# A new order for the opening of an attention-and-feed-forward kernel: five blank matmuls of full width and the six small ones taken out, copies shared anew between ScalarE and VectorE, keys of pair 2 turned before those of pair 1, and the first load of w_in held on other rows

## The chip, the cores and the metric

The kernel runs on one core of one Trainium2 chip. The metric is the device time of one execution in microseconds (us); a kernel's time is the median of several executions.

## The reference

The inputs q, k and v have 4 batches, 8 heads, 768 positions and 64 channels. Each query sees the keys nearer than 16 positions, and beside them one summary key and value for each of the 24 blocks of 32 positions. The result of attention, 3072 tokens by 512, goes through two matrix products with a swish between them.

```python
k_sum = k.reshape(B, H, nb, 32, D).max(axis=3)
v_sum = v.reshape(B, H, nb, 32, D).mean(axis=3)
scores_l = where(|i - j| < 16, scale * q @ k.T, -1e9)
scores_s = scale * q @ k_sum.T + log(32)
a = softmax(concat([scores_l, scores_s], -1))
x = (a @ concat([v, v_sum], 2)) -> (B * S, H * D)       # 3072 x 512
h = x @ w_in                                            # 512 x 2048
out = (h / (1 + exp(-beta * h))) @ w_out                # 2048 x 512
```

## The kernel before

**Units.** The eight heads are four pairs g = 0..3; the two heads of a pair lie on the two halves of the 128 partitions. Keys and queries are needed with the channel on the partitions, so they are turned. The tiles kT (keys), qn (queries), km (summary keys), e (exponentials) and xT (the result, turned) are in bf16. The 64-position tile m of the queries meets 96 keys around it and the 24 summary keys, on 120 of 128 partitions, so one exponential (L437) covers both parts of the softmax. The values are in two layouts: ve begins each tile of 128 rows 16 positions earlier than the tile, and vo holds the same rows shifted by 64. A product of e with ve or vo, one column of which is ones, gives the values and the sum by which they are divided (normalization, L527 and L528). After that x is turned (L535), multiplied with w_in (tile w_in_sb, result h in h_sb after the swish on ScalarE), and h with w_out.

**Stages.** Four batches follow one another. Attention of batch b + 1 is spread between the matmuls of batch b. Only the attention of batch 0 has nothing to hide behind. It is the *head* of the kernel, some 30 us, and does the first 384 positions (u = 0) of all four pairs and the scores of the other half (u = 1); the values of that other half come later, between the matmuls (`av0`).

**The order in the head** is written out by hand in the list HEAD: each entry is one step, and a step's instructions go to the end of their engine's queue in the order of the list. Each engine works through its own queue and waits for what an instruction needs. The steps:

- `blank n w`: n matmuls of zeros, w columns wide, into bank one[1] (L727). They compute nothing.
- `kt g x`, `qt g x`: 16 small transposes of the keys or queries of pair g into bank x (L374). `kc g e`, `qc g e`: the copy of the turned rows into kT or qn; the engine e is 'a' ScalarE (L358), 'd' VectorE (L361) or 'p' GpSimd (L364).
- `km g`: the maximum over each block of 32 keys, on VectorE (L351).
- `vc g e`: the cast of the loaded rows of v (tile vst) to bf16 in ve (L446). `vu g e`, `vl g e`: small copies from ve into vo, of 64 and of 32 rows.
- `sm g x`: seven matmuls for the summary values. `mc g e`: their copy into vm_one.
- `sc g u x`: the scores (L405 the summary keys, L407, L412 the tiles of 64, L416). `ex g u`: the exponential.
- `av g x`: the values of u = 0 (L509 with vm_one, L515 with ve and vo). `no g`: normalization. `xt g x`, `xc g e`: turning x and its copy into xT.
- `wi i`: the load of the i-th quarter of w_in, 512 columns, on GpSimd's DMA queue (L321). `begin`: the first matmuls with w_in (L568). `silu`: the load of ScalarE's table for the swish (L730).

**Loads in the head.** The rows of k and q are loaded on GpSimd's DMA queue, which turns them to bf16 on the way (krow, qrow): the heads of pair 0, of pair 1, and of pairs 2 and 3 together. Those of v go on SyncE's queue. `behind(a, b)` makes the load a wait until the load b has landed: v of pair 1 stands behind the third load of k, and the first quarter of w_in behind v of pair 1 (`vl[1]`).

**The order after the head.** The matmuls of the feed-forward part are a list of steps, `main`; everything beside it is put in by the table AT. Its numbers are positions in `main`: 6.199 means after step 6 of that list, in the order of the fractions. `av0` holds the values of batch 0's other half (pairs 0 and 1, then 2, then 3), `hs0` and `hs1` to `hs3` the sums of parts of h (tile s_sb, L635) that the second product needs (it is done by seven products in place of eight, so sums of h and w_out are formed on VectorE), `mk` the masking of the exponentials, `sc` the scores, `av` the values, `exp` and `silu` the table loads.

## Time and profile before

| what | value |
|---|---|
| time, median of 3 runs | 218.96 us (218.94, 218.96, 219.5) |
| the profiled execution, its own time | 219.06 us |
| its span, first to last instruction | 217.4 us |
| granted TensorE clock, mean | 1.0 |
| TensorE matmul (PE) busy | 205.4 us, 94% |
| TensorE weight load (PEld) busy | 141.9 us, 65% |
| VectorE (DVE) busy | 140.7 us, 65% |
| ScalarE (ACT) busy | 119.4 us, 55% |
| GpSimd (POOL) busy | 61.1 us, 28% |
| chain that ended last, by engine | PE 52%, DVE 21%, DMA 7%, SyncE's queue 6%, ACT 5%, issue 4%, POOL 3% |

Times in the rows of the trace are microseconds from the start of the span. A row of a timeline has the start, the busy time of the row, the engine, the source line, the operation, the tile written and the tile read with their shapes, and the number of instructions that the row holds. In square brackets stands the idle time of the engine ahead of the row and what ended it. In the chain of waits each row is one step of the work that ended last, followed back from the end. The blank matmuls count as busy time of TensorE, so the 94% says nothing on useful work in the head.

### The profile page before, as it was taken

The page shows a single profiled execution, that of the slowest core. Times are in us where ns is not written, and L with a number is a line of the kernel's source. Part 1 is how long each engine was busy: PE and PEld are TensorE (multiplying, and loading weights), DVE is VectorE, ACT ScalarE, POOL GpSimd, SP SyncE. Part 2 cuts the span into 40 slices and gives each one's busy share as a digit, 9 for nine tenths or more (in the row PEclk, how much of TensorE's full clock was granted, in tenths as well). Part 3 has the DMA queues.
Part 4 walks back from the last instruction along what each step waited for, and adds up shares of the span by engine and source line. Part 5 has one row for each costly group of instructions (what it writes and reads, how often), then busy time and mean ns, then how long its engine had stood idle before and what let it go on. Part 6 is the DMA issues. An engine that isn't in the chain of part 4 may idle for free.

```text
span 217.4 us, 5803 instructions
## 1 busy us (share of the span) xinstructions
PE 205.4 (94%) x2407; PEld 141.9 (65%) x2407; DVE 140.7 (65%) x323; ACT 119.4 (55%) x183; POOL 61.1 (28%) x93
## 2 busy tenths in 40 slices
PE   7978989899998899999999899999999999999993
PEld 2457756566544477556788785566878865568882
DVE  4286753599956995277899950599979713363222
ACT  2235777558669511676876143967981409663210
POOL 7617393001260004535240116163510110000111
PEclk9999999999999999999999999999999999999999
DMA  6999979999837999999959979999950740000242
GB/s 123 189 232 158 207 102 181 203 207 216 152 103 190 234 167 186 250 214 181 197 106 281 187 187 259 222 205 206 146 152 18 159 132 0 0 0 3 97 96 100
DMA packets 78394, 33.93 MB, mean 156 GB/s; under 512 B 60688, under 2 KB 75424, under 8 KB 78368
## 3 DMA queue, kind: packets, MB, share of 16 engines
q1 hardware_dynamic: 61968, 23.92, 52.2%
q0 software_dynamic: 7424, 7.34, 21.2%
q10 hardware_dynamic: 8976, 2.30, 7.0%
q8 instruction: 19, 0.31, 0.6%
q14 instruction: 7, 0.06, 0.1%
HBM read 27.37 MB, written 6.29 MB: 155 GB/s over the span
## 4 chain that ended last, share of the span: by engine, by line
PE 52%; DVE 21%; DMA 7%; SPq 6%; ACT 5%; issue 4%; POOL 3%; DVEq 0%; POOLq 0%
PE big L590 18%; PE one L654 9%; PE acc L654 7%; DMA kT<-kn 5%; PE big L568 4%; PE one L727 4%; DVE e L441 4%; DVE kw L361 2%; ACT e L437 2%; SPq L562 2%; DVE w_out_sb L327 2%; DVE qn L361 2%; DMA kst<-in_k_dram 2%; PE one L605 2%; DVE xn L528 2%
## 5 line engine op out<-in xcount | busy, mean ns | idle before, releaser
L590 PE MATMUL big<-xT,w_in_sb 128*128 128x384 bf16 x360 | 60.5, 326 | 0.0
L590 PEld LDWEIGHTS <-w_in_sb 128*128 128x128 bf16 x384 | 37.5, 98 | 25.1 <-issue 0.7
L601 ACT ACTIVATE h_sb<-big,beta_sb 128x768 bf16<-128x768 f32 x45 | 39.6, 904 | 25.9 <-PE big L590 25.8
L654 PEld LDWEIGHTS <-h_sb 128*128 128x128 bf16 x320 | 30.8, 98 | 4.5
L635 POOL TENSOR_TENSOR o_sb<-p,u 128x256 f32<-128x256 f32 x10 | 7.3, 727 | 90.0 <-DVE u L635 75.1
L437 ACT ACTIVATE e<-big,bias 128x768 bf16<-128x768 f32 x32 | 27.4, 900 | 6.6 <-PE big L416 4.5
L654 PE MATMUL one<-w_out_sb,h_sb 128*128 128x256 bf16 x240 | 30.2, 273 | 0.1
L654 PEld LDWEIGHTS <-s_sb 128*128 128x128 bf16 x240 | 23.1, 98 | 2.9
L635 DVE TENSOR_TENSOR s_sb<-h_sb 128x768 bf16<-128x768 bf16 (+2 forms) x16 | 8.5, 529 | 21.8 <-ACT h_sb L601 21.7
L635 DVE TENSOR_TENSOR u<-one,p 128x256 f32<-128x256 f32 x20 | 8.4, 420 | 14.9 <-PE one L654 14.7
L446 POOL CAST ve<-vst 128x832 bf16<-128x832 f32 (+1 forms) x15 | 13.3, 900 | 15.3 <-DMA vst<-in_v_dram 12.8
L358 ACT COPY o_sb<-one 128x256 f32<-128x256 f32 (+1 forms) x14 | 6.1, 434 | 19.1 <-PE one L654 10.1
L441 DVE TENSOR_TENSOR e<-e,mask 128x768 bf16<-128x768 bf16 x24 | 13.4, 586 | 3.5 <-ACT e L437 3.2
L605 PE MATMUL one<-w_out_sb,h_sb 128*128 128x512 bf16 x64 | 15.2, 381 | 0.0
L355 POOL COPY kw<-km 128x288 bf16<-128x288 bf16 x12 | 7.6, 636 | 20.5 <-DVE km L347 14.3
L351 DVE TENSOR_REDUCE km<-kT 128x24 bf16<-128x768 bf16 x12 | 11.3, 943 | 2.7 <-ACT kT L358 2.7
L528 DVE TENSOR_TENSOR xn<-big,r 128x768 bf16<-128x768 f32 (+1 forms) x14 | 12.6, 900 | 0.5
L568 PE MATMUL big<-xT,w_in_sb 128*128 128x384 bf16 x64 | 11.6, 327 | 0.8 <-ACT xT L358 0.8
L727 PE MATMUL one<-blank 128*128 128x512 bf16 (+1 forms) x32 | 10.0, 457 | 1.3 <-DVE blank L230 1.3
L558 POOL CAST qn<-qst 128x768 bf16<-128x768 f32 x8 | 7.5, 944 | 12.9 <-DMA qst<-in_q_dram 6.8
L654 PE MATMUL acc<-t_sb,h_sb 128*128 128x256 bf16 x80 | 10.9, 273 | 0.0
L820 ACT ACTIVATE h_sb<-big,beta_sb 128x384 bf16<-128x384 f32 x16 | 8.3, 578 | 4.4 <-PE big L568 4.4
(149 smaller groups left out, 316.2 us busy)
## 6 DMA issues: line engine op xcount, KB each, us to landing
out_dram<-o_sb SPq DMA_DIRECT2D x19, 256.0 KB, 2.7
vst<-in_v_dram SPq DMA_DIRECT2D x13, 336.0 KB, 4.8
kst<-in_k_dram SPq DMA_DIRECT2D x8, 384.0 KB, 5.3
qst<-in_q_dram SPq DMA_DIRECT2D x8, 384.0 KB, 4.9
w_in_sb<-in_moe_w_in_dram POOLq DMA_DIRECT2D x4, 512.0 KB, 8.2
w_out_sb<-in_moe_w_out_dram POOLq DMA_DIRECT2D x4, 512.0 KB, 12.7
vo<-ve SPq DMA_DIRECT2D x12, 107.2 KB, 2.3
vst<-in_v_dram SPq DMA_DIRECT2D x3, 416.0 KB, 7.3
```

What stands on the lines that cost most here:

```text
L351: nc.vector.tensor_reduce(out=km[g][:, NK:NK + nb], in_=kT[g][:, W:W + S].rearrange("p (n f) -> p n f", f=block), op=ALU.max, axis=AX.X)
L437: nc.scalar.activation(out=e[:], in_=s[:, :, 0:HS], func=ACTF.Exp, bias=bias[:, 0:1], scale=scale)
L441: nc.vector.tensor_mul(out=e.rearrange("p h (m q) -> p h m q", q=QT), in0=e.rearrange("p h (m q) -> p h m q", q=QT), in1=(mask2 if b > 1 e ...
L446: eng.tensor_copy(out=ve[:, g, lo:hi, 0:D], in_=vst[g][:, lo:hi])
L528: nc.vector.tensor_mul(out=x[:, 3 * us[0]:3 * us[0] + 3 * n].rearrange("p (k j) h d -> p k (j h) d", k=n), in0=tv[:, :, :, 0:D], in1=r[:, ...
L568: nc.tensor.matmul(t[:, 0:HS], w_in_sb[:, ki, i * P:(i + 1) * P], xT[:, ki, 0:HS], start=(ki == 0), stop=(ki == k1 - 1))
L590: nc.tensor.matmul(o, w_in_sb[:, ki, i * P:(i + 1) * P], x, start=(ki == 0), stop=(ki == k1 - 1))
L601: nc.scalar.activation(out=o, in_=t, func=ACTF.Silu, scale=beta_sb[:, i:i + 1])
L605: nc.tensor.matmul(t[:, 0:hi - lo], h_sb[:, n, ms * P:(ms + 1) * P], w_out_sb[:, n, lo:hi], start=(n == 0), stop=(n == k2 - 1))
L635: eng.tensor_tensor(out=o, in0=a, in1=b, op=op)
L654: nc.tensor.matmul(SLOTS[n], a[:, j, t * P:(t + 1) * P], b[:, j], start=(j == 0 and n not in (2, 3, 7)), stop=(j == J2 - 1), skip_group_ch ...
L727: nc.tensor.matmul(t, blank[:, 0:P], blank[:, 0:t.shape[-1]], start=True, stop=True)
```

## The change

The list HEAD is written anew, some fifty numbers of AT change, and the loads of the head get a table of their order (FIRST) and of what each held load stands behind (HOLD). The computation and the sizes of all instructions that remain are the same, but for one cast of v (pair 3): its first part, 7 of 13 columns, moves from VectorE to GpSimd.

```diff
 AT = {
...
-    'av0': [1.99, 3.682, 6.199],
+    'av0': [1.99, 3.661, 4.754],
...
-    'hs0': [34.279, 36.98, 42.604, 40.178],
+    'hs0': [36.284, 36.98, 42.604, 40.783],
...
 HEAD = [
-    ('blank', 9, 512), ('beta',), ('blank', 5, 512), ('kt', 0, 0), ('kc', 0, 'a'), ('km', 0), ('blank', 6, 512),
-    ('kt', 1, 1), ('kc', 1, 'a'), ('blank', 6, 512), ('kt', 2, 6), ('blank', 2, 256), ('kc', 2, 'd'), ('kt', 3, 6),
-    ('vc', 0, 'p'), ('vu', 0, 'd'), ('qt', 0, 2), ('kc', 3, 'a'), ('sm', 0, 7), ('mc', 0, 'a'), ('vl', 0, 'p'),
-    ('km', 1), ('qc', 0, 'd'), ('vc', 1, 'p'), ('qt', 1, 5), ('km', 2), ('blank', 2, 256), ('sc', 0, 0, 0),
-    ('vu', 1, 'p'), ('wi', 0), ('ex', 0, 0), ('qc', 1, 'd'), ('sc', 1, 0, 1), ('blank', 2, 256), ('qt', 2, 5),
-    ('qt', 3, 0), ('ex', 1, 0), ('qc', 2, 'd'), ('av', 0, 2), ('qc', 3, 'a'), ('km', 3), ('no', 0), ('sc', 2, 0, 2),
-    ('sc', 0, 1, 0), ('ex', 0, 1), ('sm', 1, 6), ('mc', 1, 'a'), ('vl', 1, 'd'), ('xt', 0, 7), ('vc', 2, 'd'),
-    ('ex', 2, 0), ('av', 1, 6), ('no', 1), ('xc', 0, 'd'), ('sc', 3, 0, 2), ('sm', 2, 6), ('wi', 1),
-    ('vc', 3, 'p', 7, 13), ('vl', 2, 'a'), ('ex', 3, 0), ('mc', 2, 'd'), ('sc', 1, 1, 0), ('vc', 3, 'd', 0, 7),
-    ('vu', 2, 'a'), ('ex', 1, 1), ('wi', 2), ('xt', 1, 4), ('xc', 1, 'd'), ('av', 2, 7), ('sc', 2, 1, 2), ('wi', 3),
-    ('ex', 2, 1), ('no', 2), ('sm', 3, 2), ('mc', 3, 'a'), ('sc', 3, 1, 0), ('ex', 3, 1), ('vu', 3, 'd'),
-    ('vl', 3, 'p'), ('xt', 2, 5), ('xc', 2, 'a'), ('av', 3, 3), ('begin', 1, 0, 3), ('no', 3), ('begin', 0, 0, 2),
-    ('xt', 3, 1), ('silu',), ('xc', 3, 'a'), ('begin', 0, 2, 3),
+    ('blank', 6, 512), ('beta',), ('blank', 3, 512), ('kt', 0, 5), ('kc', 0, 'a'), ('km', 0), ('blank', 7, 512),
+    ('blank', 5, 512), ('kt', 2, 4), ('kt', 1, 3), ('kc', 2, 'd'), ('kt', 3, 5), ('kc', 1, 'a'), ('km', 1),
+    ('qt', 0, 1), ('kc', 3, 'a'), ('vc', 0, 'p'), ('qc', 0, 'd'), ('vu', 0, 'd'), ('vc', 1, 'p'), ('sm', 0, 6),
+    ('mc', 0, 'a'), ('vl', 0, 'p'), ('qt', 1, 5), ('qc', 1, 'd'), ('sc', 0, 0, 0), ('sc', 1, 0, 1), ('ex', 0, 0),
+    ('km', 3), ('km', 2), ('qt', 2, 5), ('ex', 1, 0), ('qt', 3, 0), ('qc', 2, 'a'), ('av', 0, 7), ('no', 0),
+    ('sc', 0, 1, 1), ('vl', 1, 'd'), ('ex', 0, 1), ('wi', 0), ('qc', 3, 'a'), ('sm', 1, 6), ('sc', 2, 0, 2),
+    ('ex', 2, 0), ('mc', 1, 'd'), ('vc', 2, 'd'), ('vu', 1, 'p'), ('av', 1, 6), ('xt', 0, 7), ('vu', 2, 'a'),
+    ('no', 1), ('sc', 3, 0, 0), ('ex', 3, 0), ('wi', 1), ('sm', 2, 6), ('xc', 0, 'a'), ('vl', 2, 'a'),
+    ('sc', 1, 1, 0), ('wi', 2), ('sc', 2, 1, 1), ('vc', 3, 'p', 0, 7), ('mc', 2, 'd'), ('vc', 3, 'p', 7, 13),
+    ('vl', 3, 'p'), ('ex', 1, 1), ('xt', 1, 6), ('wi', 3), ('av', 2, 7), ('xc', 1, 'd'), ('ex', 2, 1), ('vu', 3, 'd'),
+    ('no', 2), ('sm', 3, 0), ('sc', 3, 1, 2), ('xt', 2, 7), ('xc', 2, 'a'), ('ex', 3, 1), ('mc', 3, 'd'), ('silu',),
+    ('av', 3, 6), ('no', 3), ('begin', 0, 0, 2), ('xt', 3, 1), ('xc', 3, 'a'), ('begin', 1, 0, 3), ('begin', 0, 2, 3),
 ]
+FIRST = [('k', 0, 2), ('k', 2, 4), ('k', 4, 8), ('q', 0, 2), ('q', 2, 4), ('q', 4, 8)]
+HOLD = (None, 2, 3)
...
-    behind(vl[1], kl)
+    if HOLD[1] is not None:
+        behind(vl[1], rows0[HOLD[1]])
...
         x = load_w_in(512 * i, 512 * i + 512)
-        if i == 0:
-            behind(x, vl[1])
+        if i == 0 and HOLD[2] is not None:
+            behind(x, (vl[1:] + rows0)[HOLD[2]])
```

In HOLD the 2 is the third load of k, as before; the 3 counts three loads of v first, so the first quarter of w_in now stands behind the first load of k. The blank matmuls go from 26 of 512 columns and 6 of 256 to 21 of 512. Most lines of the code stand 10 further down after the change, so L361 before is L371 after.

The instructions of VectorE in the head, from the first key maximum to the first normalization; before (tile written, then tile read, then the shape; the numbers behind a name are buffers, and the digit in kT0 to kT3, km0 to km3, qn0 to qn2 is the pair):

```order
L351 TENSOR_REDUCE km0_127<-kT0_123 128x24
L361 COPY kT2_125<-one0_78 128x768
L361 COPY vo_121<-ve_120 64x2x3x64
L351 TENSOR_REDUCE km1_128<-kT1_124 128x24
L361 COPY qn0_177<-big1_80 128x768
L351 TENSOR_REDUCE km2_129<-kT2_125 128x24
L361 COPY qn1_178<-big2_81 128x768
L361 COPY qn2_179<-big2_81 128x768
L351 TENSOR_REDUCE km3_130<-kT3_126 128x24
```

and after:

```order
L361 TENSOR_REDUCE km0_127<-kT0_123 128x24
L371 COPY kT2_125<-big2_81 128x768
L361 TENSOR_REDUCE km1_128<-kT1_124 128x24
L371 COPY qn0_177<-big0_85 128x768
L371 COPY vo_121<-ve_120 64x2x3x64
L371 COPY qn1_178<-big2_81 128x768
L361 TENSOR_REDUCE km3_130<-kT3_126 128x24
L361 TENSOR_REDUCE km2_129<-kT2_125 128x24
```

The key maxima of pairs 2 and 3 stand behind the copy of queries 1, the v copy behind queries 0, and the copy of queries 2 has left VectorE for ScalarE.

GpSimd's queue from the first cast of v to the last load of w_in; before (vst0, vst1, vst3 are the loaded rows of v of pairs 0, 1, 3):

```order
L446 CAST ve_120<-vst0_91 128x13x64
L364 COPY vo_121<-ve_120 32x2x3x64
L446 CAST ve_120<-vst1_92 128x13x64
L364 COPY vo_121<-ve_120 64x2x3x64
L321 DMA w_in_sb_183<-in_moe_w_in_dram 128x4x512 x2
L446 CAST ve_120<-vst3_94 128x6x64
L321 DMA w_in_sb_183<-in_moe_w_in_dram 128x4x512 x2
L364 COPY vo_121<-ve_120 32x2x3x64
```

and after:

```order
L456 CAST ve_120<-vst0_91 128x13x64
L456 CAST ve_120<-vst1_92 128x13x64
L374 COPY vo_121<-ve_120 32x2x3x64
L331 DMA w_in_sb_183<-in_moe_w_in_dram 128x4x512
L374 COPY vo_121<-ve_120 64x2x3x64
L331 DMA w_in_sb_183<-in_moe_w_in_dram 128x4x512 x2
L456 CAST ve_120<-vst3_94 128x7x64
L456 CAST ve_120<-vst3_94 128x6x64
L374 COPY vo_121<-ve_120 32x2x3x64
L331 DMA w_in_sb_183<-in_moe_w_in_dram 128x4x512
```

The small copy of pair 0 (32 rows) stands behind the cast of pair 1, the whole cast of pair 3 is on this engine, and the fourth load of w_in stands behind it.

VectorE between the masks (L441, after the change L451) and the first normalizations of batch 1; before:

```order
L441 TENSOR_TENSOR e_1306<-e_1306,mask_111 128x768
L441 TENSOR_TENSOR e_1339<-e_1339,mask_111 128x768
L635 TENSOR_TENSOR s_sb_1322<-h_sb_182 128x8x128
L441 TENSOR_TENSOR e_1354<-e_1354,mask_111 128x768
L527 RECIPROCAL r_1395<-big1_80 128x12
L528 TENSOR_TENSOR xn_1394<-big1_80,r_1395 128x768
L527 RECIPROCAL r_1423<-big2_81 128x12
L528 TENSOR_TENSOR xn_1422<-big2_81,r_1423 128x768
L635 TENSOR_TENSOR s_sb_1322<-s_sb_1322,h_sb_182 128x8x128
```

and after:

```order
L451 TENSOR_TENSOR e_1324<-e_1324,mask_111 128x768
L451 TENSOR_TENSOR e_1343<-e_1343,mask_111 128x768
L537 RECIPROCAL r_1383<-big1_80 128x12
L538 TENSOR_TENSOR xn_1382<-big1_80,r_1383 128x768
L537 RECIPROCAL r_1411<-big2_81 128x12
L538 TENSOR_TENSOR xn_1410<-big2_81,r_1411 128x768
L645 TENSOR_TENSOR s_sb_1305<-h_sb_182 128x8x128
L645 TENSOR_TENSOR s_sb_1305<-s_sb_1305,h_sb_182 128x8x128
```

The first sum for s_sb stands behind two normalizations in place of ahead of them.

More of the change, by code (lines that the diff above doesn't have):

```diff
@@ L13 @@
     'first': [-2.097, 0.853, -1.457, 0.459, 0.237, 1.035, 1.122, 1.113],
-    'loads': [2.388],
-    'av0': [1.99, 3.682, 6.199],
-    'x0': [5.765, 6.52],
-    'scale': [8.171, 16.158, 21.179, 21.634],
+    'loads': [2.306],
+    'av0': [1.99, 3.661, 4.754],
+    'x0': [5.759, 6.564],
+    'scale': [8.171, 16.158, 16.833, 21.634],
     'clear': [6.428, 6.644],
-    'kt': [9.534, 8.68],
+    'kt': [10.122, 8.68],
     'km': [17.109, 13.223, 16.831, 23.85],
     'qt': [26.508, 26.967],
-    'late': [32.92],
@@ L232, with row_load @@
     nc.vector.memset(vst[0][:, JV - 1], 0.0)
-    load_v(0, 0)
-    sw_load(krow, k, 0, 0, 2)
+    rows0 = []
+    def row_load():
+        nm, lo, hi = FIRST[len(rows0)]
+        rows0.append(sw_load(*{"k": (krow, k), "q": (qrow, q)}[nm], 0, lo, hi))
+    row_load()
+    v0 = load_v(0, 0)
+    if HOLD[0] is not None:
+        behind(v0, rows0[HOLD[0]])
     identity = const.tile([P, P], bf16, name="identity")
     make_identity(nc, identity)
-    sw_load(krow, k, 0, 2, 4)
+    row_load()
     band = head.tile([P, QT], bf16, name="band")
@@ L257 @@
     nc.vector.memset(As, 1.0 / block)
-    kl = sw_load(krow, k, 0, 4, 8)
+    row_load()
     select(off[:], -1, [[1, NK + QT]], -1, NEG)
```

84 lines of the change are left out of this document (42 added, 42 removed).

## The prediction

> **What bounds the kernel now.** I read the chain of waits first. It is TensorE's for 52% of the span and VectorE's for 21%, and after 43 us it is dense TensorE work with short breaks. The head, up to the first matmuls with w_in at 29.1 us, is the one long stretch where TensorE does not carry the kernel's own work all the time, and almost the whole change lies there. So the question is how much sooner the head ends, and how much of that the rest keeps. The chain begins so (start, duration, engine, tile, line, count):
>
> ```profile
> 1.26 4.02 PE one L727 x9
> 5.28 0.22 PE one L314
> 5.50 1.84 PE one L727 x5
> 7.33 0.46 PE big L374 x16
> 7.80 1.40 PE one L727 x6
> ```
>
> Blank matmuls (L727) stand on the chain itself. The first nine take 0.447 us each, the later six 0.233: the clock was at half until about 6.8 us (five in 1.84 are about three at 0.45 and two at 0.23), after 5.5 us of nearly unbroken work. Next the chain goes to VectorE, whose timeline has
>
> ```profile
> 11.56 0.96 DVE L361 COPY kT<-one 128x768 bf16<-128x768 bf16 x1 [1.94 <-PE one L374]
> 12.55 0.25 DVE L361 COPY vo<-ve 64x384 bf16<-64x384 bf16 x1
> 12.84 0.95 DVE L351 TENSOR_REDUCE km<-kT 128x24 bf16<-128x768 bf16 x1
> 13.71 0.95 DVE L361 COPY qn<-big 128x768 bf16<-128x768 bf16 x1
> 14.57 0.94 DVE L351 TENSOR_REDUCE km<-kT 128x24 bf16<-128x768 bf16 x1
> 15.43 0.95 DVE L361 COPY qn<-big 128x768 bf16<-128x768 bf16 x1
> ```
>
> That is the key copy of pair 2, v rows, key maximum of pair 1, queries 0, key maximum of pair 2, queries 1, back to back; the second scores on TensorE wait for the last of them. TensorE's timeline and then ScalarE's:
>
> ```profile
> 16.43 0.34 PE L405 MATMUL big<-qn,km 64*128 64x384 bf16 x2 [0.94 <-DVE qn L361]
> ```
>
> ```profile
> 17.25 0.90 ACT L437 ACTIVATE e<-big,bias 128x768 bf16<-128x768 f32 x1 [0.82 <-PE big L416]
> 18.38 0.80 ACT L358 COPY qn<-big 128x768 bf16<-128x768 bf16 x1 [0.23 <-PE big L374]
> 20.48 0.90 ACT L437 ACTIVATE e<-big,bias 128x768 bf16<-128x768 f32 x1 [1.30 <-PE big L416]
> 21.41 0.26 ACT L358 CAST vm_one<-one 32x128 bf16<-32x128 f32 x1
> 22.62 0.51 ACT L358 COPY vo<-ve 32x384 bf16<-32x384 bf16 x1
> 23.47 0.90 ACT L437 ACTIVATE e<-big,bias 128x768 bf16<-128x768 f32 x1 [0.34 <-PE big L416]
> 26.55 0.90 ACT L437 ACTIVATE e<-big,bias 128x768 bf16<-128x768 f32 x1 [0.72 <-PE big L416]
> 28.57 0.47 ACT L358 COPY xT<-big 128x384 bf16<-128x384 bf16 x1
> 29.05 1.28 ACT L730 ACT_TABLE_LOAD   x1
> 31.08 0.48 ACT L358 COPY xT<-big 128x384 bf16<-128x384 bf16 x1 [0.53 <-PE big L535]
> ```
>
> From the third exponential (20.48) to the table load (29.05) ScalarE idles for only 0.34 and 0.72 us: it paces the second half of the head. The last xT copy at 31.08 releases the dense matmuls.
>
> **The change, part by part.** All sums are made against the profiled execution, 219.06 us (span 217.4 and 1.66 around it); the median of the three runs is 218.96, 0.10 less, so a difference is simply taken from the median too.
>
> *Blanks and keys.* Now six blanks, beta, three blanks, then keys 0. From 1.26 that is 10 x 0.43 or a little less, to about 5.4 us. The loads that the turns need:
>
> ```profile
> 1.36 0.80 POOL L193 DMA_DIRECT2D krow<-in_k_dram  x1 [0.85 <-POOLq L943]
> 2.70 1.36 POOL L193 DMA_DIRECT2D krow<-in_k_dram  x2
> ```
>
> ```profile
> krow<-in_k_dram POOLq DMA_DIRECT2D x1, 192.0 KB, 4.7
> krow<-in_k_dram POOLq DMA_DIRECT2D x1, 384.0 KB, 6.2
> ```
>
> The second fence is from the page of DMA issues, with the time to landing. Rows for pair 0 land at 1.36 + 4.7 = 6.1, so TensorE is empty from 5.4 to 6.1, which it never was before; rows for pairs 2 and 3 land at 3.4 + 6.2 = 9.6. Keys 0 are turned at 6.1, then come twelve blanks, then keys 2. How long these take hangs on when the clock rises, and no row shows a head with that hole. Lower end: at 6.8 as before. Twelve at 0.233 end near 9.6, keys 2 (0.46) are turned by 10.2. Upper end: another 5.5 us of unbroken work counted from 6.1, so 11.6. Keys 0 take twice 0.46, to 7.0; then 10.3 blanks at 0.447 to 11.6 and 1.7 at 0.233 to 12.0; keys 2 are turned by 12.6. VectorE's copy of keys 2, at 11.56 before, thus starts at 10.2 to 12.6. I take the middle, because the hole is short beside the work around it but not nothing.
>
> The Trainium skill, "TensorE: Matmul & The Clock Gate", Part 1, says that activity is judged in free-running windows of about 3.4 us and that one busy window opens the gate; with the trace's opening at 6.8, which agrees with it, the next chance would be 10.2, keys 2 would be turned by 11.9, and the sum below would be -2.6 in place of -2.8.
>
> *VectorE's list.* From that copy to the second scores it was 16.43 - 11.56 = 4.87 us. The key maximum of pair 2 (0.86 from start to start) moves behind queries 1; the v copy's 0.29 no longer fills the wait for ScalarE's copy of keys 1 and is added to the list. So 4.3 us; the second scores start at 14.5 to 16.9. Before, TensorE needed 18.38 - 16.43 less the removed small blanks, about 1.7 us, for these scores and the turns of queries 2 and 3. Then come the values of pair 0 and the next scores. The chain prices such values, later in the head, at
>
> ```profile
> 24.91 0.18 PE one L509 x6
> 25.10 0.31 PE one L515 x12
> ```
>
> so 0.5, and scores take 0.82 to release ScalarE (16.43 to 17.25): the third exponential could start 3.0 us after the second scores, 17.5 to 19.9. It no longer waits for queries 2, since the scores of pair 0's other half now stand ahead of those of pair 2.
>
> *GpSimd's list, an added wait.* Its timeline:
>
> ```profile
> 8.86 0.50 POOL L364 COPY vo<-ve 32x384 bf16<-32x384 bf16 x1
> 15.48 0.88 POOL L446 CAST ve<-vst 128x832 bf16<-128x832 f32 x1 [6.12 <-DMA vst<-in_v_dram]
> 16.88 1.50 POOL L321 DMA_DIRECT2D w_in_sb<-in_moe_w_in_dram  x2
> ```
>
> The small copy for pair 0 (8.86) now stands behind the cast of pair 1, which waits for its load until 15.48. It ends at 15.48 + 0.88 + 0.5 and some issue, 17.0; the values of pair 0 on TensorE wait for it, and behind them every later instruction of TensorE. The third exponential therefore can't start before about 17.0 + 0.2 + 0.82 = 18.1. Range 18.1 to 19.9 against 20.48: -2.4 to -0.6.
>
> *ScalarE's list* from there to the table load had six exponentials, two of 0.26, two of 0.51, one of 0.47, and the 1.06 idle: 8.57. It now has six exponentials (5.3 in a row), queries 3 (0.80), two of 0.51, two of 0.47: 8.1, and waits of which I keep half, 0.5. So no change. After the table load the last xT copy waited 0.53 for TensorE; the values that it needs now stand further ahead, so it follows at once: -0.5. Head: -2.9 to -1.1, taken as -2.0.
>
> *w_in held on rows.* Nothing: the old wait, for the load of pair 1, is met anyway by the cast that stands ahead on the same queue, so the first part starts at 17.0 (16.88 before). It took
>
> ```profile
> w_in_sb<-in_moe_w_in_dram POOLq DMA_DIRECT2D x1, 512.0 KB, 5.4
> ```
>
> and lands at 22.4, four microseconds before its first use; without that cover each later microsecond would count. The fourth part goes behind both casts of pair 3 and is needed only from the thirteenth of the sixteen column blocks. The second batch of rows and w_out start some 3 us sooner, since GpSimd no longer waits for VectorE's part of that cast: hidden.
>
> *In the body* three places move (TensorE, VectorE, the waits, then ScalarE and TensorE late in the run):
>
> ```profile
> 41.50 0.34 PE L850 MATMUL one<-identity,xn 128*128 128x128 bf16 x3 [0.64 <-DVE xn L528]
> ```
>
> ```profile
> 72.55 0.69 DVE L635 TENSOR_TENSOR s_sb<-h_sb 128x1024 bf16<-128x1024 bf16 x1
> ```
>
> ```profile
> PE big L501 <- DVE xn L528: 0.6, 1, 0.6
> ```
>
> ```profile
> 153.09 0.35 ACT L358 COPY p<-one 128x256 f32<-128x256 f32 x1
> 153.34 1.70 ACT L437 ACTIVATE e<-big,bias 128x768 bf16<-128x768 f32 x2
> 154.62 1.04 PE L654 MATMUL one<-w_out_sb,h_sb 128*128 128x256 bf16 x8
> ```
>
> The last upper values of batch 0 are computed more than one step sooner (6.199 to 4.754), so the 0.64 goes: -0.6 (0 to -0.8). The sum s_sb that stood ahead of a normalization that TensorE waits 0.6 for now stands behind two of them: -0.5 (0 to -0.6). The copy of p moves behind two exponentials and ends near 155.1 where its bank is written again at 154.62: +0.3 (0 to 0.5). The rest (other positions in the table, the later mask turn, two transposes on SP) has its inputs long before anyone waits: nothing. Body: -0.8.
>
> Sum: -2.0 - 0.8 = **-2.8**, 216.3 for the profiled execution and **216.2** for the median; ends -3.7 and -1.9, 215.3 and 217.1.
>
> **The rivals.**
>
> *The clock rises late.* If the hole costs more than the 5.5 us counted above and the head is at half speed until about 15 us, the turns of keys 2, keys 3 and queries cost 0.46 more each and the blanks another 0.3. Some 1.0 of that lies on the path beyond the late end: -0.9, 218.0. For it: TensorE has a hole for the first time. Against it: twelve blanks follow without a break.
>
> *The clock falls again: slower.* Between the last of the twelve blanks and the first scores TensorE now carries turns of keys and queries and seven small matmuls only; before, three pairs of small blanks stood between them. If that stretch counts as idle, the clock is halved behind it, at about 13.6, and does not rise while the work stays thin. By stretches (length, TensorE busy):
>
> ```profile
> 13.62:17.03 3.41, 2.47 (x60) 1.88 (x57) 2.76 (x4) 1.48 (x3) 1.48 (x3) 1.00 1.33 222
> 17.03:20.44 3.41, 3.30 (x99) 2.75 (x94) 2.36 (x4) 1.70 (x2) 2.08 (x4) 1.00 0.82 128
> ```
>
> At half speed the busy time doubles; the idle 0.94 and 0.11 take some of it: +1.5 and +3.2 at most, half of that where ScalarE and VectorE set the pace. So +3.5 for the two stretches: 219.7. It decides from two stretches on; one alone, +1.5 at most, leaves 217.7 or less. Against it: the clock column stays at 1.00 where TensorE idled 0.94 in one stretch. For it: nothing of the trace shows turns alone.
>
> The Trainium skill says on the same page, Part 4, that transposes do not count as busy the way other matmuls do; by that the stretch is nearly idle, and the time would be this rival's. No row here shows it alone.
>
> *The head's gain is not kept.* If later loads do not start sooner, w_out and the second rows meet their users and only the body's -0.8 stays: 218.1. GpSimd's earlier start speaks against it.
>
> *Nothing happens*, since the blanks only filled waits for loads: 219.0. The chain shown first speaks against it: blanks stand on it, and the turns of keys stand between them without a wait for a DMA.
>
> **How the numbers follow.** Forecast 0.68 (215.3 to 217.1); late clock 0.12 (218.0); falling clock 0.14 (219.7, or more if it lasts); gain not kept 0.04 (218.1); nothing 0.02. A measurement here tells 0.3%, 0.66 us, from no change, so faster is below 218.3 and slower above 219.6. Faster: 0.68, 0.12, and 0.01 of the fourth, which lies near the line: 0.81. Within: the other 0.03 of the fourth and the nothing, 0.05. Slower: the falling clock, 0.14. The range goes from 215.0 (the early end with the body at its best) to 218.2, which takes in the late clock.
>
> **What would show it.** Key copy of pair 2 on VectorE between 10.2 and 12.6; second scores between 14.5 and 16.9; third exponential no earlier than 18.1, with TensorE waiting for GpSimd's copy; table load at 26.7 to 28.5; no wait at L850 at all; a short new wait at L654 near 150. Twelve blanks in 2.8 us mean the early clock, 4.3 the middle, 5.4 the late one. Scores of 64-wide tiles at twice their length after 13.6 would be the falling clock. The forecast is wrong if the table load comes within 0.5 us of 29.05, or if breaks of over 0.5 us appear after 45 us that were not there.

## The result and the profile after

| | before | after |
|---|---|---|
| time, median | 218.97 us (218.94 to 219.5, 4 runs) | 216.54 us (216.18 to 217.42, 4 runs) |
| ratio, 95% interval | | 0.9889 (0.9859 to 0.992) |
| profiled execution, its own time / its span | 219.06 / 217.4 us | 216.33 / 214.6 us |
| first swish of h on ScalarE | 32.13 us | 30.20 us |
| first turn of keys of batch 1 | 44.28 us | 41.53 us |

The forecast was 216.2 us with a range of 215.0 to 218.2. The medians differ by 2.43 us, where 2.8 was forecast, and the interval of the ratio lies clear of 1. Between the two profiled executions 2.73 us went: 1.93 up to the first swish, where -2.0 was forecast, and 0.80 behind it, where -0.8 was forecast. The head on each engine, first TensorE (a row has start, busy time, engine, line, operation, tiles and count; in brackets the idle time ahead of it):

```profile
4.15 1.46 PE L737 MATMUL one<-blank 128*128 128x512 bf16 x3
5.99 0.85 PE L384 MATMUL big<-identity,krow 96*64 96x96 bf16 x16 [0.38 <-DMA krow<-in_k_dram]
6.77 4.30 PE L737 MATMUL one<-blank 128*128 128x512 bf16 x12
11.00 0.87 PE L384 MATMUL big<-identity,krow 96*64 96x96 bf16 x32
...
15.77 0.34 PE L415 MATMUL big<-qn,km 64*128 64x384 bf16 x2 [0.37 <-DVE qn L371]
...
17.57 0.22 PE L525 MATMUL one<-ve,e 96*64 96x65 bf16 x1
17.76 0.19 PE L525 MATMUL one<-vo,e 96*64 96x65 bf16 x1
...
18.05 0.34 PE L415 MATMUL big<-qn,km 64*128 64x384 bf16 x2
```

The hole ahead of keys 0 is there, 0.38 us (0.7 was forecast), and the twelve blanks took 4.30 us, the value named for a clock that rises between the two bounds: it rose at 9.9 us, where before had 6.8. VectorE:

```profile
11.57 0.96 DVE L371 COPY kT<-big 128x768 bf16<-128x768 bf16 x1 [2.91 <-PE big L384]
12.74 0.95 DVE L361 TENSOR_REDUCE km<-kT 128x24 bf16<-128x768 bf16 x1 [0.21 <-ACT kT L368]
13.61 0.95 DVE L371 COPY qn<-big 128x768 bf16<-128x768 bf16 x1
14.59 0.26 DVE L371 COPY vo<-ve 64x384 bf16<-64x384 bf16 x1
14.76 0.95 DVE L371 COPY qn<-big 128x768 bf16<-128x768 bf16 x1
```

The copy of keys 2 starts at 11.57, before at 11.56: in this execution the blanks brought nothing at all. What the head gained begins behind it, with a list that is one key maximum shorter: the second scores came 0.66 us sooner (16.43 before). From them to the third exponential it took 3.10 us in place of 4.05, another 0.95; there the scores of pair 0's other half now stand ahead of those of pair 2, and the copy of queries 2 is on ScalarE. GpSimd and ScalarE:

```profile
16.27 0.88 POOL L456 CAST ve<-vst 128x832 bf16<-128x832 f32 x1 [7.46 <-DMA vst<-in_v_dram]
17.21 0.50 POOL L374 COPY vo<-ve 32x384 bf16<-32x384 bf16 x1
```

```profile
18.87 0.90 ACT L447 ACTIVATE e<-big,bias 128x768 bf16<-128x768 f32 x1 [0.70 <-PE big L426]
...
26.46 0.48 ACT L368 COPY xT<-one 128x384 bf16<-128x384 bf16 x1 [1.12 <-PE one L545]
26.83 0.91 ACT L447 ACTIVATE e<-big,bias 128x768 bf16<-128x768 f32 x1
27.76 1.28 ACT L740 ACT_TABLE_LOAD   x1
29.05 0.20 ACT L740 ACTIVATE dummy<-bias 128x1 f32<-128x1 f32 x1
29.16 0.46 ACT L368 COPY xT<-big 128x384 bf16<-128x384 bf16 x1
```

GpSimd's small copy ended at 17.71, and the first matmul that reads vo started at 17.76, so TensorE waited some 0.2 us for it. The third scores (18.05) follow 0.34 us behind the end of the copy and the third exponential 0.82 behind them, so in this execution the copy set the third exponential. It came 1.61 us sooner than before, the table load 1.29, the last xT copy 1.92. In the body, ScalarE and TensorE at the copy of p:

```profile
149.77 1.67 ACT L447 ACTIVATE e<-big,bias 128x768 bf16<-128x768 f32 x2
151.34 0.37 ACT L368 COPY p<-one 128x256 f32<-128x256 f32 x1
```

```profile
151.76 1.03 PE L664 MATMUL one<-w_out_sb,h_sb 128*128 128x256 bf16 x8 [0.17 <-ACT p L368]
```

The waits at the turn of the last upper values (0.64 us before) and for the normalization in batch 1 (0.6) are gone; this one is new. Of the runs below, head_only and vl0_first had one slow execution each (220.48 and 220.78 us), which is in their medians but not in their ratios.

### The profile page after: what moved, and what is told of

It is laid out like the page before. It is cut to its first block, busy times and chain, and to the rows that moved or that the text cites. A ratio compares the mean times of both kernels' runs of the same rounds, so it can differ in the third digit from the quotient of the medians.

```text
span 214.6 us, 5777 instructions
## 1 busy us (share of the span) xinstructions
PE 204.1 (95%) x2391; PEld 141.4 (66%) x2396; DVE 138.5 (65%) x322; ACT 119.5 (56%) x183; POOL 61.6 (29%) x94
## 4 chain that ended last, share of the span: by engine, by line
PE 64%; DVE 20%; ACT 10%; issue 3%; DMA 2%; DVEq 0%; POOLq 0%
PE big L600 27%; PE one L664 11%; PE acc L664 8%; ACT e L447 5%; PE big L578 4%; DVE e L451 3%; DVE kw L371 3%; DMA krow<-in_k_dram 2%; PE one L737 2%; PE one L600 2%; DVE w_out_sb L337 2%; DVE km L357 2%; PE one L615 2%; DVE qn L371 2%; PE big L384 2%
## 5 line engine op out<-in xcount | busy, mean ns | idle before, releaser
L645 DVE TENSOR_TENSOR s_sb<-h_sb 128x768 bf16<-128x768 bf16 (+2 forms) x16 | 7.8, 488 | 23.5 <-ACT h_sb L611 23.5
L645 DVE TENSOR_TENSOR u<-one,p 128x256 f32<-128x256 f32 x20 | 8.4, 421 | 15.6 <-PE one L664 14.5
L456 POOL CAST ve<-vst 128x832 bf16<-128x832 f32 (+2 forms) x16 | 13.9, 889 | 14.4 <-DMA vst<-in_v_dram 14.4
L451 DVE TENSOR_TENSOR e<-e,mask 128x768 bf16<-128x768 bf16 x24 | 13.1, 574 | 3.8 <-ACT e L447 3.7
L615 PE MATMUL one<-w_out_sb,h_sb 128*128 128x512 bf16 x59 | 14.2, 379 | 0.7 <-issue 0.6
L361 DVE TENSOR_REDUCE km<-kT 128x24 bf16<-128x768 bf16 x12 | 11.2, 944 | 3.1 <-ACT kT L368 3.1
L538 DVE TENSOR_TENSOR xn<-big,r 128x768 bf16<-128x768 f32 x12 | 11.5, 957 | 0.4
L664 PE MATMUL one<-t_sb,s_sb 128*128 128x256 bf16 x80 | 10.4, 273 | 0.0
L664 PE MATMUL acc<-t_sb,s_sb 128*128 128x256 bf16 x80 | 10.4, 273 | 0.0
L664 PE MATMUL acc<-w_out_sb,s_sb 128*128 128x256 bf16 x80 | 10.4, 273 | 0.0
```

The lines of the kernel that those rows point to most:

```text
L361: nc.vector.tensor_reduce(out=km[g][:, NK:NK + nb], in_=kT[g][:, W:W + S].rearrange("p (n f) -> p n f", f=block), op=ALU.max, axis=AX.X)
L451: nc.vector.tensor_mul(out=e.rearrange("p h (m q) -> p h m q", q=QT), in0=e.rearrange("p h (m q) -> p h m q", q=QT), in1=(mask2 if b > 1 e ...
L456: eng.tensor_copy(out=ve[:, g, lo:hi, 0:D], in_=vst[g][:, lo:hi])
L538: nc.vector.tensor_mul(out=x[:, 3 * us[0]:3 * us[0] + 3 * n].rearrange("p (k j) h d -> p k (j h) d", k=n), in0=tv[:, :, :, 0:D], in1=r[:, ...
L615: nc.tensor.matmul(t[:, 0:hi - lo], h_sb[:, n, ms * P:(ms + 1) * P], w_out_sb[:, n, lo:hi], start=(n == 0), stop=(n == k2 - 1))
L645: eng.tensor_tensor(out=o, in0=a, in1=b, op=op)
```

## The experiments

Twelve kernels were run, each beside runs of the kernel before on the same chip. The median of before there was 218.74 us for the first four of the table, 218.73 for the next four and 218.24 for the last four, so ratios are compared, not microseconds. Single executions of one kernel lie up to 1 us or more apart, so where a trace has the answer it decides: "against the first swish" means that the distance between two instructions is compared in two traces, which takes the head out of it.

| kernel | median us (executions) | ratio to before, 95% interval |
|---|---|---|
| head_only | 217.57 (12) | 0.9941 (0.9917 to 0.9964) |
| body_only | 217.84 (12) | 0.9966 (0.9948 to 0.9984) |
| av0_late | 218.18 (12) | 0.9977 (0.9944 to 1.001) |
| ssb_early | 217.34 (12) | 0.9951 (0.9925 to 0.9977) |
| blanks_old | 216.19 (7) | 0.9906 (0.9869 to 0.9943) |
| blanks_10 | 215.77 (6) | 0.9878 (0.9856 to 0.9899) |
| blanks_0 | 216.83 (6) | 0.992 (0.9893 to 0.9947) |
| km2_late | 218.14 (12) | 0.9981 (0.9955 to 1.0006) |
| sc3_old | 215.58 (4) | 0.9863 (0.983 to 0.9896) |
| small | 216.23 (6) | 0.9904 (0.9871 to 0.9938) |
| vl0_first | 216.55 (6) | 0.9895 (0.986 to 0.993) |
| best | 216.79 (6) | 0.9916 (0.9883 to 0.9948) |

### Head and body apart

**head_only**: the new HEAD and HOLD, all numbers of AT as before.

> The new HEAD and HOLD with the old table AT, so only the head is changed. Theory: the head ends 1.9 us sooner and all of it is kept, since the later loads move with it; the first swish of h (32.13 before, 30.20 after) comes at 30.2 and the time is 219.0 - 1.9 = 217.1 us. The 0.64 us wait at the turn of the last upper values stays. Rival (the head's gain is not kept, the body's places make the difference): 218.2 or more, with new waits for w_out or the second rows. Second rival (head and body need each other): below 216.7 or above 217.6.

The first swish came at 30.45, 1.68 us sooner than before, but the last products only 1.25 sooner. Two of the old places show as waits again, and one is new. TensorE's waits from 36 to 80 us, then VectorE in batch 2:

```profile
PE one L860 <- DVE xn L538: 0.6, 1, 0.6
PE big L511 <- DVE xn L538: 0.6, 1, 0.6
```

```profile
116.54 0.63 DVE L496 COPY vo<-vm_sb 32x768 bf16<-32x768 bf16 x2
117.71 0.63 DVE L496 COPY ve<-vm_sb 32x768 bf16<-32x768 bf16 x2 [0.54 <-DMA vo<-ve]
```

VectorE waits 0.54 us for the DMA that fills vo in batch 2, the masks behind it come later, and TensorE waits 1.29 us for them at 121.7, where it waited 0.67 in before and 0.20 in after. Of that 0.43 is left at the end. Neither before nor after has VectorE's wait. So both theory and rival hold in part: most of the head's gain is kept, and some of it needs the new places in the body.

**body_only**: the old HEAD, all numbers of AT as after.

> The old HEAD with the new table AT. Theory: the wait of 0.64 us at the turn of the last upper values goes (-0.8 with its surroundings), the wait for the normalization in batch 1 goes (-0.55, of which 0.2 comes back), and the copy of p behind two exponentials costs 0.3 to 0.5: together -0.8, 218.2 us. Rival (the head's gain is not kept): about 216.5, the body alone does it all. Rival (the values can't be early without the earlier head): 219.0.

The ratio is worth 0.74 us, and against the first products with w_in the end of the trace came 0.65 us sooner. That is the theory; the values of batch 0 can be early without the earlier head. The two ratios, -1.29 and -0.74 us of 218.74, give -2.0 together where after had -2.4: near a sum, with intervals of some 0.4 to 0.5 us to either side of each.

**av0_late** and **ssb_early** put one number of AT back in the kernel after.

```diff
-    'av0': [1.99, 3.661, 4.754],
+    'av0': [1.99, 3.661, 6.199],
```

> After, with the last upper values of batch 0 back at 6.199. Theory: the wait of 0.64 us for the normalization at the turn comes back, 216.5 + 0.7 = 217.2 us, and everything behind it shifts by the same. Rival (that wait had been hidden by the first keys of batch 1): 216.5.

```diff
-    'hs0': [36.284, 36.98, 42.604, 40.783],
+    'hs0': [34.279, 36.98, 42.604, 40.783],
```

> After, with the first sum for s_sb back ahead of the normalizations (34.279). Theory: TensorE waits 0.6 us for a normalization in batch 1 again at about 71 us; of that 0.2 is given back at 80 us, so +0.35, 216.9 us. Rival (VectorE only shifts the wait to the next normalization or the product with s_sb): 216.5 within 0.1.

The waits of TensorE from 36 to 80 us, av0_late and then ssb_early:

```profile
PE one L860 <- DVE xn L538: 0.6, 1, 0.6
```

```profile
PE big L511 <- DVE xn L538: 0.6, 1, 0.6
```

Each has its own wait back and not the other's. Against the first swish the first keys of batch 1 came 0.82 us later in av0_late; in ssb_early the products of batch 1 started 0.58 later, of which 0.18 was given back two products on, so 0.40 stayed. Both are the theory's sizes. By the ratios the two cost more against after, 1.9 and 1.4 us, with about 1 us to either side; their executions lie up to 3.2 us apart and after was not run beside them, so what is beyond the traces stays open.

**sc3_old** puts the scores of batch 3 back, by which the copy of p stands ahead of the two exponentials.

```diff
-    'sc3': [100.954, 100.964, 104.012, ...
+    'sc3': [101.002, 101.01, 104.012, ...
```

> After, with the first two scores of batch 3 back at 101.002 and 101.01, so that ScalarE copies p ahead of the two exponentials at about 150 us again. Theory: the wait of 0.17 us at the product that writes the bank again goes, and with it all that the start of batch 3's attention lost against before, 0.45 us: 216.1 us, the last products 0.3 to 0.45 sooner against the first swish. Rival (the late copy is covered and the loss is of another place): no change of the distance between the first swish and the last products.

ScalarE and TensorE, the same place as shown of after:

```profile
149.71 0.35 ACT L368 COPY p<-one 128x256 f32<-128x256 f32 x1
149.96 1.70 ACT L447 ACTIVATE e<-big,bias 128x768 bf16<-128x768 f32 x2
```

```profile
151.25 1.04 PE L664 MATMUL one<-w_out_sb,h_sb 128*128 128x256 bf16 x8
```

The wait is gone, and against the first swish these products came 0.45 us sooner and the last ones 0.47. This one place of the change was a loss, shown by undoing it.

### What the head gained from

**km2_late** makes one change to the kernel before.

```diff
-    ... ('km', 1), ('qc', 0, 'd'), ('vc', 1, 'p'), ('qt', 1, 5), ('km', 2), ('blank', 2, 256), ...
+    ... ('km', 1), ('qc', 0, 'd'), ('vc', 1, 'p'), ('qt', 1, 5), ('blank', 2, 256), ...
-    ... ('qc', 1, 'd'), ('sc', 1, 0, 1), ...
+    ... ('qc', 1, 'd'), ('km', 2), ('sc', 1, 0, 1), ...
```

> Before, with one change: the key maximum of pair 2 behind the copy of queries 1 on VectorE. Theory (VectorE's list is what the head gained from, not the blanks): second scores 0.86 us sooner, at 15.6 in place of 16.43, the third exponential at 19.6 in place of 20.48, 218.1 us. Rival (ScalarE or the copy of queries 2 sets the third exponential): the second scores come sooner and the third exponential stays near 20.5, 218.9.

The second scores came at 15.51 (16.43 before) and the third at 18.14 (19.05). The third exponential came at 20.21, only 0.27 sooner, because TensorE stood still inside the third scores:

```profile
18.14 0.32 PE L405 MATMUL big<-qn,km 64*128 64x384 bf16 x1
18.78 0.33 PE L405 MATMUL big<-qn,km 64*128 64x384 bf16 x1 [0.33 <-issue]
```

The second matmul of this pair waits for no semaphore, and its twin before came 0.01 us behind the first. So VectorE's list was worth 0.9 us up to there, as in theory, and the third exponential lies between theory and rival. The distance from the second to the third scores stayed as before (2.63 and 2.62 us), so what the new head gains behind the second scores is not from this. The first swish came 0.58 us sooner than before, the last products 0.24: in batch 2 VectorE waits 0.38 us for the DMA that fills vo, as in head_only. How much the time keeps is not settled (ratio 0.9981, with 1 in its interval).

**blanks_old**, **blanks_10** and **blanks_0** change only the blanks of the kernel after.

```diff
-    ('blank', 6, 512), ('beta',), ('blank', 3, 512), ... ('blank', 7, 512), ('blank', 5, 512),
+    ('blank', 9, 512), ('beta',), ('blank', 5, 512), ... ('blank', 6, 512),                     # blanks_old
+    ('blank', 6, 512), ('beta',), ('blank', 3, 512), ... ('blank', 10, 512),                    # blanks_10
+    ('blank', 6, 512), ('beta',), ('blank', 3, 512), ...                                        # blanks_0
```

> After, with the first blanks as before (nine, beta, five) and six in place of the twelve between keys 0 and keys 2. Theory: keys 0 are turned at 7.3 as before, the clock is up at 6.8, six blanks end near 9.3, TensorE then waits for the rows of pairs 2 and 3 (10.3 if they land 6.9 us after their issue) and turns keys 2 by 10.8: the key copy of pair 2 at 10.6 to 10.9 in place of 11.57, the second scores 0.7 us sooner, but the values of pair 0 are held by GpSimd's copy (17.7), so only 0.2 of it stays: 216.3 us. Rival (fewer blanks ahead of keys 0 are what brings the gain): 217.3 or more. Rival (with a wait behind the blanks the clock falls): turns at twice their length, 217.5 or more.

> After, with ten in place of the twelve blanks between keys 0 and keys 2. Theory: the blanks ran at half speed until 9.9, so ten end near 10.5 and keys 2 are turned 0.5 us sooner, at 11.1; the values of pair 0 wait for GpSimd's copy at 17.7 and take back all but 0.2: 216.4 us. Rival (keys 2 are held by their rows): no change in the turn, 216.5. Rival (the chain through VectorE keeps it all): 216.0.

> After, without the twelve blanks between keys 0 and keys 2; TensorE idles from about 6.9 until the rows of keys 2 land near 10.3. It tells what a late clock costs. Theory: the clock is not up at 9.9 and turns, copies and scores run at half speed until it rises: one more stretch of 3.4 us (rise near 13.3) +0.5 to +1.5, two (near 16.7) +2 to +3. Rival (the turns of keys and queries raise the clock as blanks do and the blanks only fill a wait): turns at full speed by 13.3 and the time within 0.5 of 216.5. Rival (they do not raise it at all): half speed until scores and values have been dense for a whole stretch, past 20 us, 219.5 or more.

With the old fourteen blanks ahead of keys 0, and twenty in all, the kernel was no slower than after: the copy of keys 2 came at 10.48, the third exponential at 18.39. So fewer blanks ahead of keys 0 are not what the gain is from, and **small** below puts the six small ones back without a loss that the time shows. In five of seven executions of blanks_old the clock fell to half for a stretch or more. In all three, TensorE now waited for the rows of keys 2, which set the floor of their turn (9.3 to 9.9 us). TensorE of blanks_10 and of blanks_0, and ScalarE's third exponential in each:

```profile
6.39 2.33 PE L737 MATMUL one<-blank 128*128 128x512 bf16 x10
9.80 0.87 PE L384 MATMUL big<-identity,krow 96*64 96x96 bf16 x32 [1.08 <-DMA krow<-in_k_dram]
```

```profile
18.38 0.90 ACT L447 ACTIVATE e<-big,bias 128x768 bf16<-128x768 f32 x1 [0.72 <-PE big L426]
```

```profile
9.26 1.49 PE L384 MATMUL big<-identity,krow 96*64 96x96 bf16 x32 [2.11 <-DMA krow<-in_k_dram]
```

```profile
18.97 0.90 ACT L447 ACTIVATE e<-big,bias 128x768 bf16<-128x768 f32 x1 [0.59 <-PE big L426]
```

How early keys 2 are copied in blanks_10 is not the two blanks alone: its clock was up at 5.2 us and ten blanks took 2.33 us, while in best (below) the same ten took 3.95.

In blanks_0 the clock rose only at 16.8 us, two stretches later than in after. The third exponential came 0.10 us later than in after and the last products 0.14, far less than the theory's +2 to +3. The time is that of the first rival, but not by its mechanism, since the turns ran at half speed. Nor is it the price of the late clock alone: without blanks keys 2 were copied 1.42 us sooner (10.15). From that copy to the second scores (15.42) it took 5.27 us in place of 4.20, so half speed cost 1.07 us on that path. Against blanks_10, whose copy came about as early (10.37), the third exponential came 0.59 us later.

**vl0_first** undoes the added wait on GpSimd.

```diff
-    ('vc', 1, 'p'), ('sm', 0, 6), ('mc', 0, 'a'), ('vl', 0, 'p'),
+    ('sm', 0, 6), ('mc', 0, 'a'), ('vl', 0, 'p'), ('vc', 1, 'p'),
```

> After, with the small copy of pair 0 back ahead of the cast of pair 1 on GpSimd. Theory: it is done by 9.5, the values of pair 0 no longer wait for it, and since they waited at most 0.2 us (17.57 to 17.76 in the trace of after) the third exponential comes 0 to 0.2 us sooner: 216.4. Rival (the added wait held the third exponential in full): it comes at 18.1 or below and the time is 215.8.

The copy was done by 9.4 and the third scores stood 0.28 us sooner than in after (17.77), of which 0.12 was there at the second scores already; the wait for the copy was thus worth 0.16, within the theory. But the third exponential came at 19.05, because TensorE stood still for 0.27 us in the middle of these scores. The time tells nothing either way (ratio 0.9895, after 0.9889). What the wait costs when the clock rises early is seen in sc3_old, whose clock was up at 4.9 us:

```profile
14.55 0.34 PE L415 MATMUL big<-qn,km 64*128 64x384 bf16 x2 [0.37 <-DVE qn L371]
...
16.07 0.36 PE L519 MATMUL one<-vm_one,e 128*128 128x65 bf16 x6
...
17.27 0.19 PE L525 MATMUL one<-vo,e 96*64 96x65 bf16 x1 [0.69 <-POOL vo L374]
...
17.55 0.34 PE L415 MATMUL big<-qn,km 64*128 64x384 bf16 x2
```

```profile
16.71 0.50 POOL L374 COPY vo<-ve 32x384 bf16<-32x384 bf16 x1
```

The second scores came 1.22 us sooner than in after, the third scores 0.50: the rest, 0.72, was spent waiting for GpSimd's copy, which ends at 17.2.

**small** puts the three pairs of small blanks back.

```diff
+    ('kt', 1, 3), ('blank', 2, 256), ... ('qc', 1, 'd'), ('blank', 2, 256), ... ('km', 2), ('blank', 2, 256),
```

> After, with the three pairs of small blanks back (behind the turn of keys 1, ahead of the first scores, ahead of the turn of queries 2). In the runs so far the new head had, in about a quarter of its executions, one stretch of 3.4 us at half clock near 12 to 16 us (mean granted clock 0.992 or below), the old head in one of 53. Theory (turns and short matmuls with gaps leave a stretch too empty, the small blanks filled it): with them no execution of twelve falls; the median is unchanged within 0.3, since VectorE sets the pace there. Rival (the falls come from the hole ahead of keys 0 and keys 2): falls in a quarter of the executions as before. Rival (each pair costs its 0.3 us on the path): 217.0.

One of six executions fell (mean clock 0.992), so that theory is refuted in its strict form; six are too few to tell one in six from a quarter. The pairs cost nothing that the time shows.

**best** joins blanks_10, vl0_first and sc3_old.

> After, with ten in place of twelve blanks, the copy of pair 0 ahead of the cast of pair 1, and p copied ahead of the exponentials. Theory: the three add up against after: -0.5 (keys 2 turned when their rows land), -0.2, -0.4: 215.3 us, a span near 213.5. Rival (the head's gain beyond this is given back where batch 1 and 2 wait for loads): 215.8.

It missed. The clock rose at 10.2 us, so ten blanks took 3.95 us, and TensorE again stood still inside the third scores, for 1.15 us:

```profile
18.04 0.37 PE L422 MATMUL big<-qn,kT 64*96 64x64 bf16 x10
19.55 0.23 PE L422 MATMUL big<-qn,kT 64*96 64x64 bf16 x2 [1.15 <-issue]
```

The gain of sc3_old's place is in it (0.47 us at the last products against the first swish), of the two others little is left: with ten blanks at that clock the copy of keys 2 came at 11.39, 0.18 us sooner than in after, and the standstill took more than both. By the ratios sc3_old and blanks_10 are the fastest, and neither is apart from after by its interval.

### The clock in the head

The mean granted clock of each execution, and where in a trace it changes, tell more than the times. In all traces it changes in steps of 3.41 us, at a phase that differs from one execution to the next. Of the traces with nine blanks ahead of keys 0, five have its first rise at 4.1 to 6.2 us (head_only, av0_late, blanks_10, sc3_old, small), four at 9.5 to 10.4 (after, ssb_early, vl0_first, best), and blanks_0 at 16.8. The stretches of head_only and then of blanks_10 that show it fall (length; busy time and count of TensorE's matmuls, weight loads, VectorE, ScalarE, GpSimd; granted clock; DMA share; GB/s):

```profile
9.61:13.03 3.42, 1.78 (x66) 1.62 (x67) 1.71 (x2) 1.14 (x2) 0.00 (x0) 1.00 1.16 201
13.03:16.44 3.41, 3.41 (x50) 2.69 (x49) 3.04 (x5) 1.28 (x3) 0.15 (x1) 0.50 1.16 224
16.44:19.85 3.41, 3.41 (x103) 2.89 (x101) 2.35 (x6) 2.79 (x5) 3.30 (x6) 1.00 0.78 136
```

```profile
8.63:12.04 3.41, 1.62 (x64) 1.43 (x64) 1.46 (x2) 0.89 (x2) 0.17 (x1) 1.00 1.17 190
12.04:15.46 3.42, 3.42 (x55) 2.67 (x51) 2.92 (x5) 1.16 (x3) 0.00 (x0) 0.50 1.30 244
```

Each time a stretch in which TensorE carried turns for 1.6 to 1.8 us of 3.41 is followed by one at half clock. Stretches that kept it are after's and sc3_old's:

```profile
9.91:13.32 3.41, 2.70 (x70) 1.80 (x67) 1.54 (x2) 0.97 (x2) 0.00 (x0) 1.00 1.22 215
```

```profile
8.30:11.71 3.41, 2.02 (x53) 1.31 (x53) 1.15 (x2) 0.80 (x1) 0.50 (x1) 1.00 1.18 186
```

Both begin with blanks (to 11.0 and to 9.1 us). The kind of work tells the two sorts apart better than how busy TensorE was. In all four traces with a fall (the other two are av0_late and blanks_old) the stretch ahead of it held turns and at most 0.32 us of other matmuls; every stretch of the head that kept the clock, in all fourteen traces, held 0.81 us of others or more. The closest pair is blanks_old, which fell after a stretch of 1.99 us with 0.32 of others, and sc3_old, which kept its clock with 2.02 us, 0.81 of them blanks. This is read from the traces; no run changed it alone. It takes an early rise: in those four the blanks ended by 8.7 to 9.1 us and TensorE waited 1.1 to 1.6 us for the rows of keys 2, while no trace with a rise at 9.4 us or later shows a fall.

Of 50 executions with the new head and its twelve blanks (after, head_only, av0_late, ssb_early, sc3_old, vl0_first) 12 have a mean clock of 0.992 or below, which is one such stretch or more (where it lies is known for the profiled ones alone); of 88 with the old head (64 of before, 12 each of body_only and km2_late) 1 has. So the new head did make the clock fall in about a quarter of its executions.

## Why the prediction was right

**The sum.** Head -1.93 against -2.0, body -0.80 against -0.8, together -2.73 against -2.8 between the profiled executions (-2.43 between the medians). The steps, by the first column as forecast and by the second as in the trace of after:

| step | forecast | trace |
|---|---|---|
| copy of keys 2 on VectorE | 10.2 to 12.6 | 11.57 |
| from it to the second scores | 4.3 | 4.20 |
| second scores | 14.5 to 16.9 | 15.77 |
| from them to the third exponential | 3.0 | 3.10 |
| end of GpSimd's small copy | 17.0 | 17.71 |
| third exponential | 18.1 to 19.9 | 18.87 |
| from it to the table load | 8.57, no change | 8.89 |
| table load to last xT copy | -0.5 | -0.63 |
| wait at the turn of the last upper values | -0.6 | -0.64, with its surroundings -0.82 |
| s_sb behind the normalizations | -0.5 | -0.55, of which 0.19 comes back |
| copy of p behind two exponentials | +0.3 | +0.45 (sc3_old) |

**Right by its mechanism:** the list on VectorE up to the second scores (km2_late), the wait at L850 (av0_late), the normalization (ssb_early), the copy of p (sc3_old), and GpSimd's added wait (sc3_old). The 0.95 us between the second scores and the third exponential have the forecast size, but no run undid the new order of the scores by itself, so that part is read from the traces.

**Luck is in the closeness of the sums.** The copy of keys 2 was put in the middle of its range with no row to say where the clock would rise. In the traces with all blanks of the new head it starts anywhere from 10.35 us (sc3_old) to 11.77 (ssb_early), and the first swish comes at 30.14 to 30.57; the old head has it at 32.13 (before) and 31.62 (body_only). So the head's gain is 1.1 to 2.0 us, depending on which traces are paired, and 1.93 is near the upper end. In the body the distance between the same swishes shrank by 0.82 us in batch 0, 0.37 in batch 1 and 0.19 in batch 2 and grew by 0.58 in batch 3, where -0.6, -0.5, 0 and +0.3 were forecast: errors that cancel.

**GpSimd's added wait** was put at a floor of 18.1 for the third exponential. The load of pair 1 was taken to land as before, at 15.48; in the fourteen traces the cast behind it starts at 15.2 to 16.4, in after at 16.27. The third exponential comes 1.2 to 1.3 us behind the end of GpSimd's small copy in after (18.87) and in four of the five runs with an early copy of keys 2 (blanks_old, blanks_10, sc3_old, small: 18.4 to 18.6); in the fifth, blanks_0, TensorE came later than that.

**Mis-sized:** ScalarE's list. Of its waits a half, 0.5 us, was kept by estimate; one wait of 1.12 us for the turn of x stands there (26.46), so the list grew by 0.32 where no change was forecast.

**Wrong in its step:** "The rest (other positions in the table ...) has its inputs long before anyone waits: nothing." head_only shows that without the new numbers of AT 0.43 us is lost in batch 2, where VectorE waits for the DMA of vo, and km2_late lost 0.26 there. With them TensorE's wait for the masks in batch 2 even fell from 0.67 to 0.20 us. Which of the numbers does it was not tried; with the last of av0 or the first of hs0 put back the wait is still 0.20. The rival that the head's gain is not kept had therefore more in it than its chance of 0.04, and was met by the new table.

**The late clock** was priced at 1.8 us above the forecast, some 1.0 of it on the path beyond the late end of the range. No run has the twelve blanks and a clock that rises as late as that. blanks_0 lost 1.07 us between the copy of keys 2 and the second scores, about what the rival counted; it did not reach the end because keys 2 came sooner without blanks.

**The falling clock** came, one stretch in each of the four traces that show it and one or more in about a quarter of the executions, where the rival counted on two. For one stretch it had named +1.5 at most. In head_only the list from the copy of keys 2 (11.11) to the second scores (15.70) took 4.59 in place of 4.20, and the third exponential came at 18.98 in place of 18.87. In head_only, av0_late and ssb_early the executions with a fall are on average within about 0.3 us of those without; in blanks_old, where five of seven fell, they took 216.9 on average and the other two 215.6; in after and small the single one that fell took 1.0 and 0.9 more. These are few runs, and none contradicts the bound. Two stretches were priced at +3.5; one execution each of av0_late (mean clock 0.982) and best (0.984), which is two stretches, took 1.0 and 0.8 us more than those without a fall. A part of the reason is that GpSimd's copy holds the third scores: in blanks_10 the fall made the list 4.72 us long, and TensorE still waited some 0.2 us for that copy, which ended at 17.22.

The Trainium skill, "TensorE: Matmul & The Clock Gate", Part 1, gives a free-running window of 3413 ns; the steps of 3.41 us and the shifting phase agree with it, and after's clock rose at 9.9, one step behind the chance at 6.5, whose stretch holds the hole (10.2 with the phase of before). The sum by that rule, -2.6, and the forecast's -2.8 lie on both sides of the -2.73 of the profiled executions, and of the two the rule's is nearer to the medians' -2.43.

The Trainium skill says on the same page, Part 4, that transposes do not count as busy in the same way. The falls agree: the stretches ahead of them held turns and at most 0.32 us of other matmuls. For the rise the runs do not decide it. In blanks_0 a stretch with 3.00 of 3.41 us of matmuls, 52 of 59 of them turns, did not raise the clock:

```profile
10.00:13.42 3.42, 3.00 (x59) 2.60 (x53) 2.64 (x3) 1.60 (x2) 0.00 (x0) 1.00 1.24 226
13.42:16.83 3.41, 3.41 (x57) 2.78 (x58) 2.87 (x5) 1.20 (x3) 1.56 (x3) 1.00 1.32 225
```

(The clock column has no entry ahead of the first rise and shows 1.00 there; the turns of keys 3 took 0.85 us where they take 0.53 at full clock.) But TensorE also stood idle for 0.42 us of it, and in after the stretch from 3.09 to 6.50 us, with 3.04 us of matmuls, most of them blanks, did not raise it either.

## What to carry to other kernels

Ask of a shortened chain what else has a fixed time of arrival: here the gain of the first half of the head ends at a load (the rows of keys 2) and at a copy that was queued behind another load's cast, and whatever is taken away ahead of them, blanks or clock, moves the end little. A falling or late clock lengthens TensorE's own list (by 0.4 us for one stretch in head_only, by 1.1 for two in blanks_0), and the end sees what goes beyond the slack to the next floor, so price it by that slack and not by the busy time that doubles. And a gain won early has to be followed to the end: with the old table a later place with a DMA of its own took back 0.43 us.

## What was not expected of the hardware

TensorE stood still with no wait shown ("issue") for 0.33 us in km2_late (0.64 between the starts of two matmuls), 0.27 in vl0_first and 1.15 in best, each time within the third scores at 18 to 19.5 us and at an instruction that waits for no semaphore. On the queue that the profile calls "instruction" one block of 16 KB had just ended, at 18.2 in best, 17.1 in vl0_first and 17.4 in km2_late; but such a block also ends at 16.5 in after and at 17.4 in before, which have no standstill there. Whether the instructions themselves came late stays open; no run separated it.
